# A register-guarded copy of h moves from GpSimd to VectorE, and two register tables load later, amid the early products

## Chip, cores and metric

One core of a Trainium2 chip runs the whole program. The metric is the device time of one execution, in microseconds; the time given is the median of the runs shown. Engines are called as in the profile: PE (TensorE), DVE (VectorE), ACT (ScalarE), POOL (GpSimd), SP (SyncE, which only issues transfers). A trailing q (POOLq, DVEq, PEldq) is the engine's sequencer, which handles branches, register loads and waits.

## What is computed

Chunked attention feeds a mixture of experts with one expert for each token:

```python
def _attn_ref(q, k, v, mem_k, mem_v):          # B, H, S, D = 4, 8, 768, 64
    for c in range(S // 32):                   # chunks of 32 queries
        k_full = concat([mem_k, k[:, :, c*32-16 : c*32+40]])   # 8 memory rows + local context
        ...
        out[:, :, c*32:(c+1)*32] = softmax(q_c @ k_full.T / sqrt(D)) @ v_full

def _moe_ref(x, w_gate, w1, w2, capacity):     # N, D, E, F = 3072, 512, 8, 1024; capacity 768
    expert_idx = argmax(x @ w_gate, axis=1)    # one expert for each token
    ...                                        # gate_w: softmax value of that expert
    h = maximum(einsum('ecd,edf->ecf', disp, w1), 0.0)
    y = einsum('ecf,efd->ecd', h, w2)
    out[i] = gate_w[i] * y[expert_idx[i], pos[i]]
```

How many tokens each expert gets is known only on the chip.

## The kernel before

**Two stages.** The first 160 us or so are attention and routing: rows of x are scattered into a DRAM buffer, x_d, in the order of experts. Then eight experts follow one after the other.

**Products in three passes.** Each fp32 matrix is held as a rounded part and a rest: w1hi and w1lo, w2hi and w2lo, xhi and xlo, hhi and hlo. A product is hi·hi + hi·lo + lo·hi. The splitting is done by ACT (the rounded part) and DVE (the rest): `split` and `split2` for weights, `trans_x` for x after its transposes on PE (L838, L842, L843), `relu` for h (L875, L876).

**One expert.** `expert(e)` runs `layer1` (h by feature block f, two blocks at a time, into the four banks `self.p1`), then `last_tile`, then `layer2` for the other token tiles. Widths and tiles that are not needed are skipped by branches on registers: `self.m[e]` is the number of 32-token blocks in the later tiles, `self.a[e]` says whether the first 256 tokens are still to be done. Where a branch skips matmuls, `instead` runs one small dummy matmul (L871). Both registers are loaded from small tables in SBUF by `values` (L793; the loads stand on L795).

**The short last tile.** A last tile with at most 64 tokens leaves half its 128 rows free. `stack` (L920) then copies the rest hlo of these 64 tokens into the free rows of hhi, so that one pass of `last_tile` (L932, L937) makes both products; otherwise eight more matmuls run (L948). The copy is done in two parts by POOL, inside a `Switch` on a POOL register: f = 0 to 5 after the relu of block pair f = 4, 5, and f = 6, 7 after that of f = 6, 7. It stands behind `split2` of the next weights in program order.

**The first expert begins early.** Before routing ends, `early` computes h for the first 256 tokens of expert 0 (L333 to L344). `expert(0)` therefore starts with their second layer, the early products: tile 0, then tile 1 with the transposes of x (`trans_x`) between its parts, while the last splits of w2 still run. `self.p2[self.order.index(t)]` gives tile 0 the bank b[0] and tile 1 the bank p1[0]. These seven banks, b, are the ones that attention and `early` used in rotation before; the four of p1 are cleared by DVE first (L774). The bank `lgp`, p2[0], serves routing and then `last_tile`. `put_y` scales the product by the gate (DVE, L959) and scatters it to the output (POOL, L960).

**Order of work.** Each engine runs its instructions in program order; the order of the code is the order of the queues. Tile dependencies become semaphore waits. SP issues the loads: x rows (`load_x`, L823), w2 of the next expert (raw2, L994), w1 of the one after (raw1, L1024).

## Time and profile before

| | us |
|---|---|
| median of 3 runs | 501.32 (500.46 to 507.27) |
| the profiled execution's own time | 505.29 |
| its span | 503.5 |
| PE busy | 463.4 (92%) |
| DVE busy | 310.7 (62%) |
| POOL busy | 119.6 (24%) |
| mean granted PE clock | 0.986 |

The profile comes from one execution. Its views used below: the share of busy time and the span in 40 slices; who waited for whom; instructions in order of time, where the bracket at the end of a row is the engine's idle time before it and what ended that; the busy time of each engine in given stretches, with the granted clock (PEclk), the DMA share and GB/s; groups of instructions by line and shape, with count, busy time and mean ns of one; and all instructions of one line with their durations (least, median, greatest, in ns) and the time of the first and the last. Time that a sequencer spends on a branch or a register load is not counted as busy.

### The profile page before, as it was taken

The page shows a single profiled execution, that of the slowest core. Times are in us where ns is not written, and L with a number is a line of the kernel's source. Part 1 is how long each engine was busy: PE and PEld are TensorE (multiplying, and loading weights), DVE is VectorE, ACT ScalarE, POOL GpSimd, SP SyncE. Part 2 cuts the span into 40 slices and gives each one's busy share as a digit, 9 for nine tenths or more (in the row PEclk, how much of TensorE's full clock was granted, in tenths as well). Part 3 has the DMA queues.
Part 4 walks back from the last instruction along what each step waited for, and adds up shares of the span by engine and source line. Part 5 has one row for each costly group of instructions (what it writes and reads, how often), then busy time and mean ns, then how long its engine had stood idle before and what let it go on. Part 6 is the DMA issues. An engine that isn't in the chain of part 4 may idle for free. (4 is left out here: it accounts for less than half of the span.)

```text
span 503.5 us, 12006 instructions
## 1 busy us (share of the span) xinstructions
PE 463.4 (92%) x4317; PEld 390.1 (77%) x4317; DVE 310.7 (62%) x676; ACT 232.0 (46%) x415; POOL 119.6 (24%) x160
## 2 busy tenths in 40 slices
PE   7899989898889985998999999999999999799993
PEld 6778877676678784887777899889988988677782
DVE  5989798998767642556645635745552685575310
ACT  6588768688442321525434415624430563443300
POOL 7621133556535341020200210010022011010011
PEclk9899999999999998899999999999999999999998
DMA  8687698987674666036470472534501644540011
GB/s 210 140 211 164 164 251 230 239 216 203 173 252 180 172 261 213 5 105 214 173 259 12 169 272 76 189 122 161 171 29 49 236 170 159 180 153 29 3 40 42
DMA packets 79393, 79.26 MB, mean 157 GB/s; under 512 B 33330, under 2 KB 60078, under 8 KB 79216
## 3 DMA queue, kind: packets, MB, share of 16 engines
q1 hardware_dynamic: 74416, 62.33, 43.3%
q0 software_dynamic: 4800, 14.95, 7.8%
q8 instruction: 65, 1.06, 0.9%
q14 instruction: 112, 0.92, 0.6%
HBM read 61.25 MB, written 15.99 MB: 153 GB/s over the span
## 5 line engine op out<-in xcount | busy, mean ns | idle before, releaser
L875 ACT ACTIVATE hhi<-ps 128x512 fp32r<-128x512 f32 x68 | 40.7, 599 | 148.8 <-PE ps L862 136.7
L876 DVE SCALAR_TENSOR_TENSOR hlo<-ps,hhi 128x512 fp32r<-128x512 f32 x68 | 47.0, 691 | 72.5 <-ACT hhi L875 69.7
L960 POOL DMA_INDIRECT out_dram<-y,tok x28 | 31.8, 1137 | 196.6 <-DVE y L959 73.6
L953 PE MATMUL ps<-w2hi,hhi 128*128 128x512 f32 x160 | 64.1, 401 | 1.4 <-DVE hlo L344 1.4
L862 PE MATMUL ps<-xhi,w1hi 128*128 128x320 f32 (+3 forms) x288 | 59.4, 328 | 5.9 <-DVE hlo L876 2.2
L953 PE MATMUL ps<-w2lo,hhi 128*128 128x512 f32 x160 | 62.9, 393 | 0.0
L953 PE MATMUL ps<-w2hi,hlo 128*128 128x512 f32 x160 | 62.5, 391 | 0.0
L862 PE MATMUL ps<-xhi,w1lo 128*128 128x320 f32 (+3 forms) x288 | 57.7, 322 | 0.0
L862 PE MATMUL ps<-xlo,w1hi 128*128 128x320 f32 (+3 forms) x288 | 57.6, 322 | 0.0
L862 PEld LDWEIGHTS ps<-xhi,w1hi 128*128 128x128 f32 x288 | 45.2, 188 | 10.4 <-ACT w2hi L853 3.7
L862 PEld LDWEIGHTS ps<-xhi,w1lo 128*128 128x128 f32 x288 | 45.9, 188 | 3.0
L862 PEld LDWEIGHTS ps<-xlo,w1hi 128*128 128x128 f32 x288 | 45.9, 188 | 2.8
L959 DVE TENSOR_SCALAR y<-ps,xg 128x512 f32<-128x512 f32 x20 | 15.0, 750 | 49.8 <-PE ps L953 45.0
L854 DVE TENSOR_TENSOR w2lo<-raw,w2hi 128x512 fp32r<-128x512 f32 x64 | 42.5, 705 | 0.0
L843 DVE TENSOR_TENSOR xlo<-ps,xhi 128x512 fp32r<-128x512 f32 x34 | 23.4, 690 | 27.2 <-ACT xhi L842 26.6
L827 DVE TENSOR_TENSOR w1lo<-raw,w1hi 128x512 fp32r<-128x512 f32 x56 | 36.6, 684 | 2.6 <-DVEq L846 0.6
L842 ACT CAST xhi<-ps 128x512 fp32r<-128x512 f32 x34 | 19.9, 587 | 38.8 <-PE ps L838 32.0
L953 PEld LDWEIGHTS ps<-w2hi,hhi 128*128 128x128 f32 x160 | 30.0, 188 | 8.6 <-DVE hlo L344 1.6
L853 ACT CAST w2hi<-raw 128x512 fp32r<-128x512 f32 x64 | 36.3, 620 | 0.0
L552 PE MATMUL ps<-vw,pT 128*32 128x130 f32 x768 | 29.2, 277 | 7.3 <-issue 3.7
L826 ACT CAST w1hi<-raw 128x512 fp32r<-128x512 f32 x64 | 35.5, 620 | 0.8
L953 PEld LDWEIGHTS ps<-w2hi,hlo 128*128 128x128 f32 x160 | 30.1, 188 | 7.0
(163 smaller groups left out, 810.3 us busy)
## 6 DMA issues: line engine op xcount, KB each, us to landing
raw<-in_moe_w_dram SPq DMA_DIRECT2D x15, 2048.0 KB
raw<-in_q_dram SPq DMA_DIRECT2D x11, 512.0 KB
raw<-in_k_dram SPq DMA_DIRECT2D x10, 512.0 KB
vw<-in_v_dram SPq DMA_DIRECT2D x49, 64.0 KB
xg<-x_d SPq DMA_DIRECT2D x3, 792.0 KB
vw<-in_v_dram SPq DMA_DIRECT2D x31, 72.0 KB
xg<-x_d SPq DMA_DIRECT2D x4, 528.0 KB
xg<-x_d SPq DMA_DIRECT2D x2, 1056.0 KB
```

The costliest lines, as they stand in the source:

```text
L552: nc.tensor.matmul(ps[32 * c4:32 * c4 + 32, i * 130:i * 130 + 130], pT[:, pr * P + 32 * c4:pr * P + 32 * c4 + 32], vw[:, c + c4 + 1, :, pr ...
L826: self.nc.scalar.copy(out=hi[sl], in_=raw[sl])
L827: (eng or self.nc.vector).tensor_tensor(out=lo[sl], in0=raw[sl], in1=hi[sl].bitcast(F32), op=ALU.subtract)
L842: nc.scalar.copy(out=self.xhi[:, d:d + k, sl], in_=pv)
L843: nc.vector.tensor_tensor(out=self.xlo[:, d:d + k, sl], in0=pv, in1=self.xhi[:, d:d + k, sl].bitcast(F32), op=ALU.subtract)
L853: self.nc.scalar.copy(out=self.w2a[:, j], in_=self.raw2[:, j])
L854: self.nc.vector.tensor_tensor(out=self.w2b[j // 4][:, j % 4], in0=self.raw2[:, j], in1=self.w2a[:, j].bitcast(F32), op=ALU.subtract)
L862: self.nc.tensor.matmul(ps, a[:, d, fs], b[:, d, o:o + w], start=(i + d == 0), stop=(i == 2 and d == KD - 1))
L875: self.nc.scalar.activation(out=self.hhi[hs], in_=ps, func=AF.Relu)
L876: self.nc.vector.scalar_tensor_tensor(out=self.hlo[hs], in0=ps, scalar=0.0, in1=self.hhi[hs].bitcast(F32), op0=ALU.max, op1=ALU.subtract)
L953: self.nc.tensor.matmul(ps, a[:, f, t * P:t * P + P], b, start=(f == 0 and i == 0), stop=(f == KF - 1 and i == 2))
L960: nc.gpsimd.indirect_dma_start(out=self.out[:, :], out_offset=bass.IndirectOffsetOnAxis(ap=tok[:, t:t + 1], axis=0), in_=y, in_offset=None ...
```

## The change

`stack` becomes a DVE copy under an `If` on a register that only DVE holds (`self.mv`, a second load of the same table), and it moves ahead of `split2`. The loads of the tables `self.m` and `self.a` move from `experts` into `expert(0)`: m behind the matmuls of early tile 0, a behind the second transposes in early tile 1. The early products use p2[0] (lgp) and p2[1] (b[0]) in place of b[0] and p1[0], and the scaling and scatter of tile 1 come before the third transposes.

```diff
 def experts(self, ctx):
-        self.m = self.values(self.m32, ENGS, 4 * nt + 1)
-        self.a = self.values(self.big, ENGS + (ET.Activation,), 2)
         self.rows = self.values(self.kind, ET.SP, 3 * TB)
 ...
 def layer1(self, e, todo2):
+            if g >= KF - 4:
+                self.stack(e, slice(0, g + 2) if g == KF - 4 else slice(g, g + 2))
             for _ in fs:
                 if todo2:
                     self.split2(todo2)
-            if g >= KF - 4:
-                self.stack(e, slice(0, g + 2) if g == KF - 4 else slice(g, g + 2))
             if g % 4:
                 self.first_rows(e, (g - 2, g))
 ...
 def stack(self, e, fs):
         o = EARLY + TB * P - P
-        for n in self.tc.Switch({ET.Pool: ((self.m[e] + 1) >> 1) & 1}, 2):
-            if n:
-                self.nc.gpsimd.tensor_copy(out=self.hhi[:, fs, o + P // 2:o + P], in_=self.hlo[:, fs, o:o + P // 2])
+        with self.tc.If((self.mv[e] + 1) & 2):
+            self.nc.vector.tensor_copy(out=self.hhi[:, fs, o + P // 2:o + P], in_=self.hlo[:, fs, o:o + P // 2])
 ...
 def expert(self, e):
-        m, a = self.m[e], self.a[e]
 ...
             tok = self.tokens(e, 0, TA)
-            for t in range(TA - 1):
-                self.layer2(e, t, tok)
-            ps = self.p2[self.order.index(TA - 1)]
-            for i, fs in enumerate((range(0, 3), range(3, 6), range(6, KF))):
-                self.mm2(ps, TA - 1, fs)
-                self.trans_x(e, i, 1)
-            self.put_y(e, ps, TA - 1, tok)
-            self.trans_x(e, KD - 1, 1)
+            self.mm2(self.p2[0], 0, range(KF))
+            self.m = self.values(self.m32, ENGS, 4 * self.nt + 1)
+            self.mv = self.values(self.m32, ET.DVE, 4 * self.nt + 1)
+            self.put_y(e, self.p2[0], 0, tok)
+            self.mm2(self.p2[1], 1, range(0, 3))
+            self.trans_x(e, 0, 1)
+            self.mm2(self.p2[1], 1, range(3, 6))
+            self.trans_x(e, 1, 1)
+            self.a = self.values(self.big, ENGS + (ET.Activation,), 2)
+            self.mm2(self.p2[1], 1, range(6, KF))
+            self.put_y(e, self.p2[1], 1, tok)
+            for d in range(2, KD):
+                self.trans_x(e, d, 1)
             self.trans_a(e)
         self.layer1(e, list(range(KF)) if e else [])
 ...
+        m, a = self.m[e], self.a[e]
```

## The prediction

> **What bounds the kernel now.** I read the busy shares first, then the granted clock, then PE's waits in the expert stage, then that place in order of time.

> ```profile
> PE 463.4 (92%) x4317; PEld 390.1 (77%) x4317; DVE 310.7 (62%) x676; ACT 232.0 (46%) x415; POOL 119.6 (24%) x160
> PEclk9899999999999998899999999999999999999998
> ```

> PE is busy 92% of the span, so time goes away only where PE stands still or runs slowly. The clock row has one dip between its ends, in the slices around 200 us. Who waited on PE, from 170 us to 500 us:

> ```profile
> PE lgp L932 <- POOL hhi L925: 6.2, 1, 6.2
> PE ps L862 <- DVE hlo L876: 2.2, 4, 1.4
> PE ps L862 <- DVE y L959: 1.5, 1, 1.5
> ```

> One wait stands out, and it is for the very copy that the change moves (L925). In order of time on PE:

> ```profile
> 194.06 0.33 PE L871 MATMUL ps<-pad 128*64 128x64 f32 x2
> 200.64 0.79 PE L932 MATMUL lgp<-w2hi,hhi 128*128 128x512 f32 x1 [6.25 <-POOL hhi L925]
> ...
> 203.22 0.77 PE L932 MATMUL lgp<-w2hi,hhi 128*128 128x512 f32 x1
> ...
> 205.74 0.48 PE L932 MATMUL lgp<-w2hi,hhi 128*128 128x512 f32 x1
> ...
> 207.10 0.48 PE L932 MATMUL lgp<-w2hi,hhi 128*128 128x512 f32 x1
> ```

> From 194.39 to 200.64 PE is empty. The next two rounds of `last_tile` (four matmuls and four transposes each) take 2.58 and 2.52 us, the third 1.36. The stretches of one us say why:

> ```profile
> 197.00:198.00 1.00, 0.00 (x0) 0.00 (x0) 0.00 (x0) 0.00 (x0) 0.00 (x0) 1.00 1.08 418
> 198.00:199.00 1.00, 0.00 (x0) 0.00 (x0) 0.00 (x0) 0.00 (x0) 0.00 (x0) 0.94 0.49 193
> 204.00:205.00 1.00, 1.00 (x3) 0.67 (x3) 0.69 (x1) 0.25 (x1) 0.00 (x0) 0.50 0.00 0
> 205.00:206.00 1.00, 1.00 (x6) 0.93 (x5) 0.00 (x0) 0.00 (x0) 0.29 (x1) 0.65 0.03 8
> ```

> The columns are PE, PEld, DVE, ACT, POOL, then clock, DMA share, GB/s. The clock was cut to 0.50 late in 198:199 (0.94 is 0.88 at full speed and 0.12 at half), so about 4.5 us after PE ran dry, and came back within 205:206.

> Why was POOL late? Its inputs were ready, since hlo of f = 5 ended at 191.97 (DVE row below). The sequencer's rows show a jump:

> ```profile
> L1048 POOLq COMPARE_BRANCH  x1: 43/43/43, 194.5 to 194.5; - x1
> L923 POOLq BRANCH_PREFETCH_HINT  x1: 43/43/43, 199.8 to 199.8; - x1
> L1048 POOLq COMPARE_BRANCH  x1: 43/43/43, 202.7 to 202.7; - x1
> L923 POOLq BRANCH_PREFETCH_HINT  x1: 43/43/43, 205.2 to 205.2; - x1
> L925 POOL CAST hhi<-hlo 128x384 fp32r<-128x384 f32 x5 | 3.2, 632 | 59.3 <-ACT w2hi L853 53.1 <-DMA raw<-in_moe_w_dram 6.2
> L925 POOL CAST hhi<-hlo 128x128 fp32r<-128x128 f32 x5 | 1.8, 355 | 23.2 <-PE ps L838 9.8 <-ACTq L912 5.0 <-DVE xlo L843 4.9
> ```

> Between the Switch's branch and the first instruction of the chosen case lie 5.3 us the first time and 2.5 us the second. The first falls under the load of w2 (418 GB/s above), the second under hardly any transfer. The copy itself takes 0.63 and 0.36 us in the mean; the stall is the jump's.

> **The change part by part.** *The copy on DVE.* DVE around that place:

> ```profile
> 191.28 0.69 DVE L876 SCALAR_TENSOR_TENSOR hlo<-ps,hhi 128x512 fp32r<-128x512 f32 x1 [1.07 <-ACT hhi L875]
> 193.04 0.69 DVE L876 SCALAR_TENSOR_TENSOR hlo<-ps,hhi 128x512 fp32r<-128x512 f32 x1 [1.07 <-ACT hhi L875]
> 194.80 0.69 DVE L876 SCALAR_TENSOR_TENSOR hlo<-ps,hhi 128x512 fp32r<-128x512 f32 x1 [1.07 <-ACTq L912]
> L498 DVE COPY kw<-kw 64x672 f32<-64x672 f32 x13 | 8.5, 651 | 2.2 <-ACT kw L481 2.1
> L500 DVE COPY kw<-kw 64x96 f32<-64x96 f32 x9 | 2.0, 217 | 0.0
> L940 DVEq ALU_OP  x16: 45/45/52, 209.1 to 475.6; - x16
> L940 DVEq COMPARE_BRANCH  x13: 41/49/69, 209.3 to 475.7; - x13
> 209.86 0.69 DVE L943 COPY y<-lgp 64x512 f32<-64x512 f32 x1
> ```

> SBUF copies of 96 and 672 elements took 0.22 and 0.65 us, so the copies of 384 and 128 lie between; I take 0.43 and 0.24 on the line through both. The branch is of the form of L940, two register operations and a branch of 0.05 us each: 0.15 us. The first copy starts at 191.97 and ends by 192.6, in the gap of 1.07 us before the next relu: 1.8 us before PE is free. The second waits for the last relu (195.49) and ends by 195.9; PE needs it three rounds of 1.36 us after its start, at 198.5. The copy waits for nothing outside DVE; behind it stands the next relu, then `split2`, which moves by 0.58 us at most and is needed only by `last_tile`. Five experts copy (ten POOL rows), eight test: 5 × 0.67 + 16 × 0.15 = 5.8 us on DVE, whose gaps for ACT (1.07 us, above) hide it. If they did not, the bound would be 5.8 us. The 6.25 us go: **−6.25**. Nothing is late next: ACT and DVE are idle in 197:199, and the transposes of the next x find their banks free since layer 1 began.

> *The clock.* With no gap there the two slow rounds take 2.72 instead of 5.10 us: **−2.38**. Bounds: 0 (the cut stays) and 2.38.

> [...]

> *Early products in other banks, tables later.*

> ```profile
> 161.86 1.11 PE L342 MATMUL ps<-xlo,w1hi 128*128 128x256 f32 x8
> 164.33 0.50 PE L953 MATMUL ps<-w2hi,hhi 128*128 128x512 f32 x1 [1.36 <-DVE hlo L344]
> 163.86 0.42 DVE L344 SCALAR_TENSOR_TENSOR hlo<-ps,hhi 128x256 fp32r<-128x256 f32 x1
> 166.06 2.48 DVE L854 TENSOR_TENSOR w2lo<-raw,w2hi 128x512 fp32r<-128x512 f32 x4
> 169.96 0.40 PE L953 MATMUL ps<-w2hi,hhi 128*128 128x512 f32 x1
> 178.89 0.59 ACT L842 CAST xhi<-ps 128x512 fp32r<-128x512 f32 x1 [1.25 <-PE ps L871]
> 179.17 0.82 PE L862 MATMUL ps<-xhi,w1hi 128*128 128x320 f32 x4 [1.46 <-DVE y L959]
> L795 PEldq TENSOR_LOAD <-m x1: 781/781/781, 162.0 to 162.0; - x1
> L795 PEldq TENSOR_LOAD <-big x1: 600/600/600, 162.9 to 162.9; - x1
> L838 PEldq EVENT_SEMAPHORE  x9: 51/51/51, 169.3 to 436.8; - x9
> L838 PEld LDWEIGHTS ps<-ident,xg x136: 137/140/226, 171.8 to 442.0; 128*128 128x128 f32 x136
> ```

> Tile 0 starts at 164.33, when the hlo of L344 that began at 163.86 ends: its first matmul needs hhi and w2hi of f = 0, not that, so it waits for the bank. In `lgp` it can start at 163.0. It then meets the four last splits of w2, which end 0.62 us apart up to 168.54: the second matmul of f = 4 waits until 166.68, and eleven at 0.235 us (24 from 164.33 to 169.96) bring tile 0's end to about 169.3 instead of 169.96: **−0.65** (bounds 0 and 1.36). Layer 1's first bank no longer waits for y of tile 1 (1.46 us). But the fourth matmul of that row reads xhi of d = 3, which ACT writes until 179.48, so only three of its four, some 0.4 us, can run ahead: **−0.4** (bounds 0 and 1.46).

> PE's loads of m and a took 0.78 and 0.60 us while L342 ran, so they don't empty PE. In their new place the sequencer is about 2.5 us ahead (it passed the wait of L838 at 169.3, the transposes ran at 171.8): 0, at worst 1.4. On DVE, ACT and POOL a load of the same kind stands before work that waits for PE anyway: 0. SP's queue is unchanged. POOL's first two scatters of y come a little later behind the loads; no PE row waits for them, and the second passes no other POOL instruction. The mv load adds no transfer queue.

> *Sum.* 6.25 + 2.38 + 0.65 + 0.4 = 9.7 us. Against the profiled execution, 505.29 (span 503.5 and 1.8 around it): 495.6. That execution lies 4.0 us above the median of the runs; the same 9.7 us off 501.32 give **491.6**. With the bounds: −6.25 alone gives 495.1, all upper ends (11.45) give 489.9.

> **The rivals.** *A. The timed runs hold less of the stall.* The 5.3 us belong to one execution, and the other jump took 2.5 us. Were it 2.5 us, 2.8 us less, PE would stand 3.4 us, under the 4.5 us after which the clock was cut. The change then brings 3.4 + 1.05: 496.8. For it: the median lies 4.0 us below the profiled execution, near the 2.8 + 2.4 that this case takes off. Against it: the jump falls under the same w2 load in each run.

> *A2. The cut misses the gap.* It came 1.8 us before PE started again; 1.8 us later in another execution, and it takes no time before the change either. Then 7.3 us go: 494.0. For it: no row ties the cut to that moment.

> *B. DVE pays the jump (slower).* If DVE's new branch stalls as POOL's did, by 2.5 to 5.3 us, twice in each of eight experts, DVE is late for xlo of the next expert; the third transposes (d = 2) need the bank of d = 0 back. In expert 0 they would run two rounds and four matmuls after 194.39, at 198.0, so the first xlo (0.7 us) must begin by 197.3, while the last relu ends at 195.49: 1.8 us of slack, some 1.25 after copy, branch and the token copy that follows. In seven experts PE loses the jump less 1.25 us, in expert 0 also the jump less 1.8 for its first copy: 8.5 + 0.7 at 2.47 (500.8), 28 + 3.5 at 5.3 (about 523). From a jump of 2.55 us on it is slower than before. Against it: the skipped body is one instruction, and after the branch at 209.3 (L940 above) DVE's L943 began at 209.86 without idle time.

> [...]

> *C. The table loads empty PE.* Then 1.05 becomes −1.4: 501.32 − 8.63 + 1.4 = 494.1. Against it: the loads at 162.0 and 162.9 beside L342.

> **How the numbers follow.** Forecast 0.52, A 0.23, A2 0.10, B 0.06, C 0.09. A run-to-run difference of 2% (10.0 us) is about what a measurement of this kernel can tell from no change. The forecast stands at 9.7, its bounds at 6.25 and 11.45, so about half of it passes 10.0, and of A, A2 and C nothing: faster 0.27. B ends beyond +2% for jumps over some 3.8 us, which is most of its chance: slower 0.04. Same 0.69. The range reaches from the upper ends, 489.9, to A's 496.8 and 1 us for how far the two closer runs lie apart: 489.9 to 497.8. It leaves out B, and of A what lies above.

> **What would show it.** Right: no idle time before the first L932 of expert 0, PEclk 1.00 around 200 us, DVE rows of 128x384 and 128x128 on the stack's line of 0.2 to 0.65 us, POOL without them; the first L953 near 163.0 with a short pause in tile 0; L862 without a wait for y. Wrong: idle time on DVE after its branch (B), a gap on PE at the loads (C), a profile that gains 9.7 us while the timed median gains 4 (A), or a new wait before `last_tile`'s transposes.

## The result, and the profile after

| | before | after |
|---|---|---|
| median, us | 500.89 (500.37 to 507.27) | 487.02 (485.95 to 489.06) |
| ratio | | 0.970, 95% interval 0.9615 to 0.9784 |
| the profiled execution's own time, us | 505.29 | 485.95 |
| its span, us | 503.5 | 484.0 |

The change saves 13.9 us in the medians, where 9.7 were forecast; 487.0 us lies below the range, and the gain is over 2%, to which the forecast gave a chance of 0.27. The ratios, here and below, leave out executions more than 1.5% above the fastest of their kernel, and the medians take all. Timed again beside before on two more occasions, each on a chip of its own, after saved 11.3 us (ratio 0.9758, 0.9706 to 0.9809) and 11.7 us (0.9786, 0.9739 to 0.9833): the gain is real, and some two to four microseconds larger than the sum of the forecast.

The busy shares and the granted clock of after, and who waited on PE from 150 to 477 us (total, times, longest):

```profile
PE 458.9 (95%) x4317; PEld 387.4 (80%) x4317; DVE 312.3 (65%) x686; ACT 231.9 (48%) x415; POOL 114.0 (24%) x150
PEclk9899999999999999999999999999999999999998
```

```profile
PE ps L860 <- DVE hlo L874: 2.1, 4, 1.4
PE ps L869 <- issue: 1.8, 2, 0.9
PE ps L860 <- ACT w2hi L851: 1.7, 1, 1.7
PE ps L860 <- issue: 0.9, 1, 0.9
```

The wait for POOL is gone from PE's list, and the clock's dip around 200 us with it. In order of time on PE, at the start of `last_tile` of expert 0 (L929 here, L932 before):

```profile
183.88 0.33 PE L869 MATMUL ps<-pad 128*64 128x64 f32 x2
184.14 0.50 PE L929 MATMUL lgp<-w2hi,hhi 128*128 128x512 f32 x1
...
185.53 0.48 PE L929 MATMUL lgp<-w2hi,hhi 128*128 128x512 f32 x1
...
186.90 0.48 PE L929 MATMUL lgp<-w2hi,hhi 128*128 128x512 f32 x1
```

No idle time stands before 184.14, and the first two rounds take 1.39 and 1.37 us instead of 2.58 and 2.52. The copy and its branch, two rows of their lines on DVE (least, median, greatest duration in ns; first and last start):

```profile
L922 DVE CAST hhi<-hlo x10: 226/293/361, 181.8 to 418.3; 128x384 fp32r<-128x384 f32 x5, 128x128 fp32r<-128x128 f32 x5
L921 DVEq COMPARE_BRANCH  x26: 43/47/63, 181.3 to 454.0; - x26
```

Ten copies of 0.23 and 0.36 us, and branches of 0.05 us without a jump behind them. So the change does what it says. What has to be explained is the size.

### The profile page after: what moved, and what is told of

Its sections match the earlier page's. It is cut to its first block, busy times and chain, and to the rows that moved or that the text cites. A ratio compares the mean times of both kernels' runs of the same rounds, so it can differ in the third digit from the quotient of the medians.

```text
span 484.0 us, 11825 instructions
## 1 busy us (share of the span) xinstructions
PE 458.9 (95%) x4317; PEld 387.4 (80%) x4317; DVE 312.3 (65%) x686; ACT 231.9 (48%) x415; POOL 114.0 (24%) x150
## 4 chain that ended last, share of the span: by engine, by line
PE 55%; DMA 16%; issue 13%; DVE 11%; ACT 1%; SPq 1%; POOLq 1%; DVEq 0%; ACTq 0%
PE ps L860 19%; DMA out_dram<-y,tok 13%; PE ps L950 13%; PE lgp L929 5%; PE ps L511 3%; PE ps L465 2%; PE ps L836 2%; PE ps L552 2%; DVE vw L417 2%; PE ps L333 2%; DVE m L519 2%; DVE d L522 1%; PE ps L477 1%; PE ps L607 1%; DVE xr L560 1%
## 5 line engine op out<-in xcount | busy, mean ns | idle before, releaser
L950 PE MATMUL ps<-w2hi,hhi 128*128 128x512 f32 x152 | 60.9, 401 | 0.0
L950 PE MATMUL ps<-w2lo,hhi 128*128 128x512 f32 x152 | 59.8, 393 | 0.0
L950 PE MATMUL ps<-w2hi,hlo 128*128 128x512 f32 x152 | 59.4, 391 | 0.0
L852 DVE TENSOR_TENSOR w2lo<-raw,w2hi 128x512 fp32r<-128x512 f32 x64 | 41.2, 685 | 0.9 <-DVEq L921 0.6
L950 PEld LDWEIGHTS ps<-w2hi,hlo 128*128 128x128 f32 x152 | 28.5, 188 | 6.7
L950 PEld LDWEIGHTS ps<-w2hi,hhi 128*128 128x128 f32 x152 | 28.5, 188 | 6.7
L481 ACT COPY kw<-ps 64x512 f32<-64x512 f32 x46 | 28.5, 620 | 11.1 <-PE ps L477 10.5
L950 PEld LDWEIGHTS ps<-w2lo,hhi 128*128 128x128 f32 x152 | 28.5, 188 | 5.8
```

The costliest lines, as they stand in the source:

```text
L481: (nc.vector.tensor_copy if n == 0 and hf else nc.scalar.copy)(out=kw[r, :, :, hf, 24 + j:56:2], in_=ps[j * 64:j * 64 + 64])
L852: self.nc.vector.tensor_tensor(out=self.w2b[j // 4][:, j % 4], in0=self.raw2[:, j], in1=self.w2a[:, j].bitcast(F32), op=ALU.subtract)
L950: self.nc.tensor.matmul(ps, a[:, f, t * P:t * P + P], b, start=(f == 0 and i == 0), stop=(f == KF - 1 and i == 2))
```

## The experiments

Each group of runs was on one chip with before timed beside it; the chips are called A to D. Stage times below are read off PE's rows. They are counted from the first matmul of `early` (first L333), called the first early product below although it stands ahead of the second-layer products that the sections above call early, because the stage ahead of it differs between chips (last group of this section).

### Chip A: the two halves apart

The stack alone is before with the DVE copy under its `If`, ahead of `split2`; tables, banks and order of the early products stay:

```diff
-        for n in self.tc.Switch({ET.Pool: ((self.m[e] + 1) >> 1) & 1}, 2):
-            if n:
-                self.nc.gpsimd.tensor_copy(...)
+        with self.tc.If((self.mv[e] + 1) & 2):
+            self.nc.vector.tensor_copy(...)
...
+        self.mv = self.values(self.m32, ET.DVE, 4 * nt + 1)    # behind self.m, early
```

The tables alone are after with POOL's `Switch` back and `stack` behind `split2` again. Beside them ran before and after, unchanged.

Expected of before: 

> The kernel before, beside after and its two halves on one chip. If the longer attention stage (early products at 147 to 151 us, DVE 4.4 us without work before L517) belongs to the chip: all four programs of this call show it or none does. If it belongs to the program: before, the stack alone and the tables alone show it here, after does not.

Expected of after: 

> The kernel after on the same chip as before and the two halves. Forecast's sizes: 9.7 us less than before. What the other profiles say: 334 to 335 us from the first early product to the end against 345 to 348 in before, so 11 to 13 us less in the median too if the attention stage is the same in both; 14 or more if that stage gains as well.

Expected of the stack alone: 

> The stack alone. If the halves add up as in the forecast: 8.6 us less than before, and after is 1 us lower still. If the halves hide each other: less than before by 7 to 9, and after lies 2 to 4 us lower, which the tables alone do not bring.

Expected of the tables alone: 

> Banks, order and later loads alone. If the halves add up: 1 us less than before (forecast) or 3 to 4 (what after has over the stack alone in the profiles). If POOL's queue sets the start of last_tile in expert 0 whatever PE does ahead of it: no gain (within 0.3%), layer 1 starts 1.5 to 3 us sooner after the early products and PE's wait before last_tile is longer by as much.

| chip A | before | tables alone | stack alone | after |
|---|---|---|---|---|
| median, us | 499.7 (beside it 499.9) | 501.2 | 488.4 | 488.3 |
| ratio | 1.0007 (0.9975 to 1.0038) | 1.0004 (0.9965 to 1.0042) | 0.9787 (0.9736 to 0.9837) | 0.9786 (0.9739 to 0.9833) |
| first early product at | 143.79 | 148.66 | 144.21 | 142.98 |
| from there to: early tile 0 | 12.62 | 12.62 | 12.64 | 12.62 |
| layer 1 of expert 0 | 27.44 | 25.82 | 27.36 | 25.80 |
| its `last_tile` | 51.60 | 53.14 | 42.32 | 40.97 |
| the tiles behind that | 60.50 | 62.05 | 48.41 | 47.06 |
| end of PE | 347.32 | 348.95 | 334.54 | 333.99 |

The stack alone has the whole gain, as far as these runs can tell, and neither expectation had its size: 8.6 or 7 to 9 us expected, 10.6 measured in the ratio and 11.6 in the medians, and after is 0.1 us lower, not 1 or 2 to 4 (the intervals of the two leave room for some 2 us). The tables, banks and order bring nothing measurable by themselves, although layer 1 starts 1.6 us sooner with them. Why not is seen in PE's waits: before, then the tables alone, then the stack alone (the rows that matter here):

```profile
PE lgp L932 <- POOL hhi L925: 9.1, 1, 9.1
...
PE ps L862 <- DVE y L959: 1.5, 1, 1.5
```

```profile
PE lgp L930 <- POOL hhi L923: 11.9, 1, 11.9
```

```profile
PE ps L872 <- issue: 2.2, 2, 1.1
PE ps L863 <- ACT w2hi L854: 1.7, 1, 1.7
PE ps L863 <- DVE y L959: 1.5, 1, 1.5
```

With the tables alone the wait for y is gone and the wait for POOL is 2.8 us longer: PE runs dry 1.3 us sooner and waits for POOL all the same. (The other 1.5 us are POOL's, in an execution of 507.3 us against a median of 501.2.) As long as POOL sets the start of `last_tile`, what PE saves ahead of it is worth nothing.

### What POOL was doing

Before on chip A, the rows of POOL's sequencer and of POOL on the lines of the scatter, the `Switch` and the copy:

```profile
L960 POOLq EVENT_SEMAPHORE  x1: 7307/7307/7307, 182.4 to 182.4; - x1
L960 POOL DMA_INDIRECT out_dram<-y,tok x1: 972/972/972, 182.5 to 182.5; - x1
L1048 POOLq COMPARE_BRANCH  x1: 43/43/43, 192.0 to 192.0; - x1
L923 POOLq BRANCH_PREFETCH_HINT  x1: 43/43/43, 194.5 to 194.5; - x1
L925 POOL CAST hhi<-hlo x1: 506/506/506, 194.8 to 194.8; 128x384 fp32r<-128x384 f32 x1
```

POOL issues the scatter of early tile 0 at 182.5 and then stands 7.3 us in a wait ahead of the scatter of tile 1. Its semaphore had its last increment from the first scatter at 189.66; the wait ended at 189.69. Only then come the branches and the `Switch`, whose jump took 2.5 us (192.0 to 194.5). PE had been empty since 186.33. The same row stood in the trace from which the forecast was made, and it was not read there:

```profile
L960 POOL DMA_INDIRECT out_dram<-y,tok x2: 969/971/973, 188.7 to 192.9; - x2
...
L960 POOLq EVENT_SEMAPHORE  x1: 3633/3633/3633, 188.5 to 188.5; - x1
```

So two things stand in series ahead of POOL's copy, the landing of a scatter and a jump. Three kernels take them away. What no kernel here takes away lies further back: y of tile 0 was ready at 163.5 on chip A, but POOL came to its scatter only at 182.5, behind the scatters of pads, a memset of 2.7 us (L782) and the `Switch` on `full` (L784).

The jump (chips B and D): before with the copy still on POOL, at its old place, under an `If` on a register of POOL's own.

```diff
-        for n in self.tc.Switch({ET.Pool: ((self.m[e] + 1) >> 1) & 1}, 2):
-            if n:
+        with self.tc.If((self.mp[e] + 1) & 2):
```

Expected on chip B: 

> The stack's copy stays on POOL, at its old place in the order, but under an If on a register of POOL's own instead of the Switch. If the jump of the Switch is the cost and not the engine: the 6.25 us go here too; POOL's copy (0.63 us) follows its relu's hlo without a pause, and the median is 8.6 us lower than before (about 492.3). If POOL itself is late for another reason (its queue, its port), PE still waits several us for it, and the median stays near 500.9.

Expected on chip D: 

> The stack's copy on POOL under an If of POOL's own instead of the Switch, a second execution, on the chip of the three below. The jump is gone, the wait of POOL for the first early scatter to land is left. If that wait ends near the time at which PE is ready: PE waits 0 to 3 us for POOL and the time is 7 to 11 us below before. If the queue alone sets the start of last_tile: PE waits 5 to 7 us as in the first execution, and the time is 2 to 4 us below before.

The landing (chip C): before, with `put_y` of the two early tiles ending ahead of its scatter.

Expected: 

> The kernel before with the scatters of the two early tiles of expert 0 left out (256 rows of the output lack one expert's part); the stack stays on POOL under its Switch. If the stall is the jump's (forecast): PE still waits 3 to 6 us for the stack's copy. If POOL is late because its queue stands behind the second early scatter, which waits until the first has landed: POOL takes the jump before the relu ends, PE does not wait for it, and the time falls by 5 to 8.6 us below before.

Both (chip D):

Expected: 

> POOL under an If, and the scatters of the two early tiles of expert 0 left out (256 rows of the output lack one expert's part): neither the jump nor the landing stands ahead of the copy. If these two are all that made POOL late: PE does not wait for POOL, the copy follows its hlo within 1 us, and the time is 11 to 12 us below before, as with the copy on DVE. If POOL is late for a third reason (its port, its own speed of 0.63 us): a wait of over 1 us stays.

| | chip | median, us | before, us | ratio | wait for the landing | PE's wait for POOL |
|---|---|---|---|---|---|---|
| no jump | B | 498.4 | 507.3 | 0.9814 (0.9765 to 0.9863) | 9.41 | 6.07 |
| no jump | D | 502.2 | 507.5 | 0.9842 (0.9798 to 0.9886) | 3.21 | 0 |
| no scatter | C | 493.9 | 499.1 | 0.9891 (0.9844 to 0.9939) | none | 2.67 |
| neither | D | 499.4 | 507.5 | 0.9849 (0.9805 to 0.9894) | none | 0 |

The two last columns belong to the profiled executions, and on chip B that one took 507.3 us, the other five 493.0 to 500.0, so its landing of 9.4 us need not be the usual one. First on B, then on D (all of the line's rows of that kind in the stretch):

```profile
L960 POOLq EVENT_SEMAPHORE  x3: 17/43/9412, 186.8 to 190.7; - x3
```

```profile
L960 POOLq EVENT_SEMAPHORE  x3: 17/43/3207, 185.8 to 188.1; - x3
L925 POOL CAST hhi<-hlo x2: 293/400/507, 195.4 to 198.9; 128x384 fp32r<-128x384 f32 x1, 128x128 fp32r<-128x128 f32 x1
```

On D the landing took 3.2 us and POOL reached the copy at 193.6, ahead of its data; the copy began when its hlo came, at 195.4, and PE waited for nothing. Without scatters but with the jump, POOL was on time for the first copy and late for the second: the jump of that one took 5.2 us (187.6 to 192.8), and PE waited 2.67 us inside `last_tile`. With neither, POOL is in time for both. POOL's own copy, 0.51 and 0.29 us here, made PE wait in neither profile on D. The 11 to 12 us expected of neither were not reached: 7.7 us in the ratio, no more than without the jump alone on the same chip (8.0). In the medians it is 8.0 against 5.3, so how the gain on D divides between jump and landing is not settled. On B the kernel without the jump brought 9.4 us in the ratio (7 to 12) and the copy on DVE 5.6 (3 to 8, below): nothing on B shows that the copy had to leave POOL. What stays open is how much the jump alone is worth on chips like A and C, where that kernel was not run; taking the jump's 2.5 us off the 9.06 us that PE waited on A leaves a wait of some 6.6 us there, an estimate.

### Chip D: a gap of chosen length on PE

The kernel after, with repeats of one split of relu on DVE ahead of the first stack copy of expert 0, six in one kernel and eleven in the other:

```diff
+            if not e and g == KF - 4:
+                for _ in range(6):      # 11 in the other kernel
+                    nc.vector.scalar_tensor_tensor(out=self.hlo[...], in0=pss[1], scalar=0.0, in1=..., op0=ALU.max, op1=ALU.subtract)
```

Expected of six: 

> The kernel after with six repeats of one split of relu (0.69 us each, the same values again) ahead of DVE's first stack copy in expert 0, which makes it 4.1 us late where PE has 1.9 us of slack: a gap of about 2.2 us on PE. Forecast (a gap under 4.5 us meets no cut of the clock): 2.2 us slower than after. If the clock goes by windows of 3.4 us of which a part is idle (cuts of 3.41 us after gaps of 2.0 to 2.7 us elsewhere): 2.2 us and, where the gap falls into one window, 1.7 us more.

Expected of eleven: 

> The kernel after with eleven such repeats: the copy is 7.6 us late, a gap of about 5.7 us on PE. If the cut of the clock costs what the forecast says (2.4 us beside the gap): 8 us slower than after. If the gap alone costs: 5.7 us. With cuts in windows of 3.41 us at half clock, two windows, of which the gap covers a part: 5.7 and 1.7 to 3.4 us.

Medians 501.1 and 506.9 us beside before's 507.5 (ratios 0.9865, 0.9817 to 0.9913, and 0.9997, 0.9964 to 1.0029). The gap with six was 1.0 us, not 2.2, since PE came late itself by an unnamed 1.4 us; with eleven:

```profile
193.04 0.33 PE L869 MATMUL ps<-pad 128*64 128x64 f32 x2
199.46 0.77 PE L934 MATMUL lgp<-w2hi,hhi 128*128 128x512 f32 x1 [6.10 <-DVE hhi L927]
```

```profile
198.00:199.00 1.00, 0.00 (x0) 0.00 (x0) 0.93 (x3) 0.00 (x0) 0.00 (x0) 0.72 1.05 414
205.00:206.00 1.00, 1.00 (x5) 0.72 (x5) 0.37 (x1) 0.58 (x1) 0.00 (x0) 0.87 0.00 0
```

(Columns as in the prediction: the clock is the third number from the end.) The clock was cut from 198.44 to 205.27, and `last_tile` took 8.73 us instead of 6.02 in the kernel with six: the cut costs 2.7 us. The two medians differ by 5.8 us, the profiles by 5.1 of gap and 2.7 of clock; the times alone can't tell 5.1 from 7.8. Over the whole expert stage the two profiles differ by only 2.5 us, since the one with six lost more elsewhere in layer 1, so the 2.7 us of the clock rest on `last_tile` itself. The kernel after was not timed on D, so neither expectation can be held against it; against before, a gap of 6.1 us put in by hand takes the kernel after back to the time of before.

### Chip C: banks and loads

After unchanged, after with the tables loaded early, and after with the early tiles in their old banks (`self.p2[1]` and `self.p2[2]`):

Expected of after: 

> The kernel after, unchanged, for a second profile beside the others. If the 8.1 us by which the attention stage was shorter in the two first profiles are spread of the executions: the early products start between 145 and 150 us here, as in three profiles with the unchanged attention code, and the gain over before is 10 to 11 us. If they belong to this program: about 142 us again and 13.9 us. In both the expert stage from the first early product to the end takes 334 us, as in the first profile of after (345 in that of before).

Expected of early tables: 

> The kernel after, but m, its copy for DVE and a are loaded ahead of expert 0 as before. If the later loads bring or cost nothing (forecast): the same as after within 0.3%. If PE's loads ahead of the early products cost time: about 1 us slower. If the loads amid the products hold PE back (rival C): up to 1.4 us faster than after, and the 0.88 us of PE without a named cause at layer 1 are gone.

Expected of old banks: 

> The kernel after, but the two early tiles use the banks of before. Forecast's size: 1.05 us slower than after. Rival 'early products are worth more': about 3 us slower (2.8 us of waits for banks, 1.3 before tile 0 and 1.5 before layer 1, and their transposes behind them).

Medians 487.8, 488.0 and 488.8 us beside before's 499.1 (ratios 0.9758, 0.9706 to 0.9809; 0.9766, 0.9706 to 0.9827; 0.9808, 0.9758 to 0.9857). In the profiles (the first of an execution of 492.3 us) layer 1 starts 26.02, 25.82 and 25.83 us after the first early product, and PE ends 334.67, 333.77 and 333.68 us after it. With the new order, neither the banks nor the place of the loads makes a difference that these runs can show: the old banks' median is 1.0 us higher, as the forecast's size would have it, but within the intervals and without a trace in the profile. What lets layer 1 start 1.6 us sooner is most likely the order, y of tile 1 ahead of the third transposes: it is the one thing that these three share and the stack alone lacks. The order by itself was not run. The 0.9 us without a named cause in the first profile of after is absent here with early and with late tables, so the loads don't make it.

### Chip B, and what the chips differ in

Before, the stack alone and the tables alone had also run on chip B.

Expected of the stack alone: 

> Only the stack's copy is moved (DVE under an If, ahead of split2); the tables load early, the early products keep their banks and order. Forecast's sizes: 6.25 of the stall and 2.38 of the clock go, so 8.6 us less than before (about 492.3), tile 0 still starts 1.36 us after the early products, layer 1 still waits 1.46 us for y. Rival 'early products are worth more' (3.2 us, as the two traces have it): the stack alone brings 13.9 - 3.2 = 10.7 or less, the same two pauses stay. Rival 'the attention stage moves with the placement of the code': the early products do not start at 150.2 us but several us sooner, with instructions that are the same there, and the median falls by more than the expert stage gains.

Expected of the tables alone: 

> Only the early products' banks and order and the later loads of the tables; the stack stays on POOL under its Switch. Forecast's sizes: 1.05 us less than before (about 499.8), within 0.3%. Rival 'early products are worth more': 3.2 us less (497.7), 1.5 of it before tile 0 of the early products and 1.6 before layer 1. In both the 6.25 us of PE before last_tile of expert 0 stay, or differ by what the jump takes in this execution, and with them the cut of the clock.

Expected of before: 

> The kernel before, unchanged, for a second profile. If the attention stage differs by the spread of executions: early products start sooner than 150.2 us here (142 to 150), and DVE's 4.4 us without work at 135 us is gone or elsewhere. If it belongs to how this program lies in memory: 150 us again, DVE's gap at 135 us again. The stall before last_tile: the forecast has about 6 us again, its rival A (the timed runs hold less of the stall) about 3.4 us and no cut of the clock.

| chip B | before | tables alone | stack alone |
|---|---|---|---|
| median, us | 507.9 (beside it 507.3) | 506.2 | 500.9 |
| ratio | 1.0014 (0.9973 to 1.0055) | 0.9989 (0.9951 to 1.0027) | 0.9889 (0.9843 to 0.9934) |
| from the first early product to: early tile 0 | 14.66 | 13.20 | 14.69 |
| layer 1 of expert 0 | 30.28 | 27.50 | 29.53 |
| end of PE | 347.66 | 347.44 | 338.42 |

Here too the tables alone bring nothing measurable and the stack does, though less: 5.6 us in the ratio. The same program takes some 8 us longer on B and D than on A and C (before: 507.3 and 507.5 against 499.1 and 499.9). DVE's waits in the attention stage, 128 to 141 us, in the stack alone on B and then the same kernel on A:

```profile
DVE ps L517 <- PE ps L535: 4.4, 1, 4.4
```

```profile
DVE rc L555 <- PE ps L552: 0.4, 2, 0.2
```

All eight profiles on B and D have this wait of 4.3 to 4.6 us ahead of a memset of L517, which the view puts down to PE's L535 in some and to no engine in others; none of the eight on A and C has it. On B and D the early tile 0 also waits 1.2 to 1.4 us for hlo of L344 where the old banks are used; on A and C it doesn't, with the same banks. The first profile of before has both marks, that of after neither: as far as these profiles tell, the 8.1 us by which the two differ ahead of the early products come from where they ran, and are no part of the change. Some of it can be the spread of executions: one on A and one on C, without the marks, reach that point only at 148.7 and 147.8 us. Each chip was used on one occasion, so chip and occasion can't be told apart.

## Why the prediction missed

**What bounds the kernel, and the place: right.** The wait for the stack's copy was the one to go, the clock's dip went with it, and nothing new came in its place. DVE's side was costed well: copies of 0.36 and 0.23 us (0.43 and 0.24 expected), branches of 0.05, no PE wait for them. Rival B (DVE pays the jump) did not happen.

**The step that failed: the size of the stall.** The forecast took 6.25 us as a fixed cost, by "the stall is the jump's". The jump was the last link of POOL's chain, and I took it for the chain: ahead of it POOL waits for the first scatter to land, 3.63 us in the one profile. PE's wait is what is left of that chain when PE gets there, and it varies from both ends. The five profiled executions of before and of the tables alone (times in us from the first early product, then durations):

| | before, first | before, B | before, A | tables, B | tables, A |
|---|---|---|---|---|---|
| POOL's first scatter of y at | 38.45 | 38.61 | 38.74 | 39.10 | 38.63 |
| PE runs dry at | 44.18 | 47.89 | 42.54 | 45.84 | 41.25 |
| wait for the landing | 3.63 | 8.72 | 7.31 | 7.61 | 8.07 |
| jump | 5.28 | 2.60 | 2.49 | 2.71 | 2.70 |
| PE's wait for POOL | 6.25 | 5.11 | 9.06 | 7.32 | 11.90 |

Before on chip B, POOL's wait for the landing and PE's first matmul of `last_tile`:

```profile
L960 POOLq EVENT_SEMAPHORE  x1: 8715/8715/8715, 185.7 to 185.7; - x1
```

```profile
200.23 0.79 PE L932 MATMUL lgp<-w2hi,hhi 128*128 128x512 f32 x1 [5.11 <-POOL hhi L925]
```

POOL's first scatter comes at nearly the same time in all five, landing and jump together take 8.9 to 11.3 us, and the time at which PE runs dry differs by 6.6 us: the longest wait is that of the earliest PE, not that of the longest landing. Chip A's 9.06 is 2.8 us more than the forecast's 6.25, 1.6 of it because PE is ready sooner and 1.2 because POOL's chain is longer (the landing 3.7 more, the jump 2.8 less, the scatter 0.3 later). On B the stack alone brought 5.6 us, less than the forecast's 8.6; the same number was too small on one chip and too large on another. Rival A went the wrong way: it took the jump's 2.5 us for a reason why the timed runs hold less of the stall. On chip A the jump was 2.5 us, as that rival supposed, and PE waited 9.06 us.

**The clock: right in kind, 2.38 forecast.** `last_tile` of expert 0 fell from 8.37 to 6.13 us (2.24) between the two first profiles and from 8.90 to 6.09 (2.81) on chip A; the gap made by hand cost 2.71. On chip B it was 1.3 (7.00 us in before, 5.66 in the stack alone, up to the dummy matmul behind it), so 2.38 is a size within a spread and no price. Rival A rested on a gap under 4.5 us escaping the cut, A2 on a cut that comes too late to cost anything. A cut followed every gap of over 5 us before `last_tile` (5.11 to 11.90 us, seven in all), and a shorter gap did not escape: in the kernel without scatters PE was idle for 2.67 us, and the clock was cut 2.5 us after it ran dry:

```profile
193.41 0.79 PE L932 MATMUL lgp<-w2hi,hhi 128*128 128x512 f32 x1 [2.67 <-POOL hhi L925]
```

```profile
192.00:193.00 1.00, 0.00 (x0) 0.00 (x0) 0.09 (x1) 0.00 (x0) 0.00 (x0) 1.00 0.00 0
193.00:194.00 1.00, 0.59 (x1) 0.50 (x2) 0.00 (x0) 0.00 (x0) 0.29 (x1) 0.61 0.02 8
196.00:197.00 1.00, 1.00 (x6) 0.67 (x6) 0.43 (x1) 1.00 (x3) 0.00 (x0) 0.68 0.02 8
```

**The early products: 1.05 forecast, no gain that the times can show.** Of the two terms one was absent on the chips where after was timed beside before again: early tile 0 does not wait for its bank on chips A and C, so 0.65 became 0. The other was larger than the 0.4 put down: layer 1 starts 1.6 us sooner. But the forecast added the halves, and they don't add. With the old stack the 1.6 us are lost in the wait for POOL. With the new one 1.35 us are left at the end of `last_tile` and 0.55 at the end of PE, and the medians of the stack alone and of after differ by 0.1. Rival C (the loads empty PE) did not happen: PE has no wait at the loads, and layer 1 starts at 25.82 us with early tables and at 25.80 and 26.02 with late ones on A and C.

**The sum.** On chip A, before to after, by the profiles: 1.64 up to layer 1, 8.99 to `last_tile`, 2.81 in it, 0.11 given back later, 13.3 together (11.7 in the medians). Against the forecast's 9.7 the stall is 2.7 more, the clock 0.4, the early products 0.6, and the rest is the 0.1. That the first comparison showed 13.9 where the later ones show 11.3 and 11.7 lies inside their intervals.

## What to carry to other kernels

When a consumer waits for an engine, read that engine's own queue back from the late instruction until it is idle for want of work: here the nearest cause in the chain was not all of it. The wait is what is left of that chain when the consumer arrives, so its size has to be worked out from both ends; the wait of one execution is not a price. A saving ahead of a wait that another engine ends is worth nothing until that wait is gone; terms on both sides of it must not be added. And a queue in which a scatter waits for the one before to land, here for 3.2 to 9.4 us, is a poor place for a copy that the bottleneck waits for.
